# Keys and queries of an attention pair fetched and transposed earlier, and batch-end work moved by one slot

## Chip, cores and metric

One core of a Trainium2 chip runs the whole program. The metric is the device time of one execution, in microseconds (us); lower is better. The kernel before took 782.35 us (median of 3 runs, 782.05 to 782.71).

## What is computed

Three layers in a row, all in float32 at the interface. The change lies in the first; the batch ends belong to the second.

```python
# q, k, v: (4, 8, 1152, 64): 4 batches, 8 heads, 1152 positions, 64 channels
q_pool = q.reshape(B, H, S // 2, 2, D).mean(axis=3)          # 576 pooled queries a head
scores = (1 / sqrt(D)) * q_pool @ k.T
attn = softmax(scores, axis=-1)
x = (attn @ v)  -> (2304 tokens, 512)
logits = x @ phi                                             # soft mixture: 8 experts, 4 slots each
slot_in = softmax(logits, axis=0).T @ x
slot_out = relu(slot_in @ w1) @ w2                           # one w1, w2 per expert
y = softmax(logits, axis=1) @ slot_out
h = y @ w_in
out = where(h >= 1, h, where(h <= -1, 0, (h + 1)**2 / 4)) @ w_out
```

## The kernel before, in words

**Pairs, steps, slots.** The 32 heads are worked in 16 pairs (P = 0 to 15), two heads of one batch at a time. A pair has NK = 9 steps, one for each 128 keys, and each step has two slots (one per head, or per half). Global step g runs from -11 to 144; pair P's scores lie in steps 9P to 9P + 8. The main loop (L705 to L721) emits for each slot, in this order: one half block of maxima (`max_half`, L296), one block of transposed scores with its exponential (`st`, L361), the sums of exponentials where they are due (`es_sum`, L388, at steps 7 and 9 after the pair's start), one product with the values (`pv`, L397), and then whatever the plan has put into that slot (`slot`, L646). The order in which instructions are emitted is the order on each engine; the framework adds the waits, and a tile in a pool with one buffer is handed on when its last reader is done.

**Maxima run ahead.** The maxima of pair P are computed 11 steps (LEAD = NK + 2) before its scores, that is from step 9P - 11, slot 0, on. PE multiplies K1[P] with q1[P] (L305), VectorE (DVE) reduces (L317), and `max_fin` (L339) turns the maxima into the rows of q2[P], transposed by a DMA (L354). PE waits at the first L305 of a pair until K1[P] and q1[P], with its copy, are in place.

**The prologue of a pair** is what the change moves. For pair P, with b = 9P, `plan` (L584) puts:

- `load_k2` and `load_q` (L219, L231): two key loads (L229) and four query loads (L237 to L240), all issued by SP, into kf and qf;
- `prep_khi` (L249): ScalarE (ACT) makes the fp16 high part of the keys, one pass per head, in kn;
- `prep_klo` (L254): DVE makes the low part, the last reader of kf;
- `prep_qp`, `prep_qhi`, `prep_qlo` (L269, L275, L282): DVE adds the two neighbours of each pooled query, ACT makes the high part in qn1, DVE the low part; `prep_qlo` is the last reader of qf;
- `xpose_k` (L263): SP issues one DMA transpose per head, kn to K1 (L266);
- `xpose_q1` (L286): one DMA transpose, qn1 to q1 (L288);
- `dup_q1` (L290): a DMA copies the upper 64 rows of q1 to the lower 64 (L291), after the transpose has landed.

kf, qf, kn and qn1 have one buffer each (pool g0, `bufs=1`); K1 and q1 have three, by P % 3. The table PREP (L44) gives the steps for two plans: entries are load step, key high step, two key low half steps, pooled query half step, query high step, query low half step, all relative to b. The first plan serves pair 2, the second all later ones; pairs 0 and 1 are started by hand (L650 to L690).

```python
 44 PREP = (-20, -18, (-34, -33), -36, -16, -30), (-24, -22, (-41, -37), -41, -19, -37)
587     lk, hk, lok, aq, hq_, loq = PREP[P > 2]
```

A half step s means step s // 2, slot s % 2: -34 is (b - 17, 0), -30 is (b - 15, 0). Within a slot, pairs are planned in rising order.

**What shares the queues.** SP issues every DMA of this stage: also the value loads (L246, step b - 8, slot 1), the fill of S2 from K1 (L294, step b - 9, slot 1), the stores and loads of the weight conversion (L209, L212, L185), q2's transposes (L354), and, at the end of every ninth step from 30 on, a weight load of 1 MB (L133). SP works in order: what waits there holds all that is queued behind.

**Batch ends.** After every fourth pair the finished tokens give logits for the mixture: `lg_part`, `lg_sum`, `lg_max`, `lg_exp`, `lg_nat` (six small PE transposes and a DVE copy), `p_mm` (products with the tokens, PE) and `p_add` (DVE), at half steps LGT (L33) after b of the pair that ends the batch; for b = 63 half step 34 is (80, 0). The last batch has its own order and isn't touched. PE's results of scores, maxima and these share three PSUM tiles (pool sc, L73).

Of the kernel before, what the change touches and what calls it, by code (L numbers as in the profile page):

```python
# [29 lines left out]
P1G = -2, -1, 0, 1, 2, 3, 4, 5, 6  # L30
TMUL = (12, 0, 0, (0, 1)), (12, 1, 0, (2,)), (12, 1, 1, (0,)), (13, 0, 1, (1, 2))
TXN = 0, 1
LGT = 30, 31, 32, 33, 34, 36, 37  # L33
LPT = 6
WPH = 3
REA = 0
# [4 lines left out]
ADD = ((4, 1, 0, 0, 2), (5, 1, 1, 0, 1), (6, 1, 1, 1, 2), (6, 2, 0, 0, 2), (7, 2, 1, 0, 2), (8, 3, 0, 0, 1), (9, 3, 0, 1, 2),  # L41
       (10, 3, 1, 0, 2), (10, 4, 0, 0, 1), (11, 4, 0, 1, 2), (12, 4, 1, 0, 1), (13, 4, 1, 1, 2))

PREP = (-20, -18, (-34, -33), -36, -16, -30), (-24, -22, (-41, -37), -41, -19, -37)  # L44


@with_exitstack
def fused_kernel(ctx: ExitStack, tc: tile.TileContext, q, k, v, phi, w1, w2, w_in, w_out, out):
# [532 lines left out]
    def at(g, slot, f, *a):  # L581
        sched.setdefault((g, slot), []).append((f, a))

    def plan(P):  # L584
        b = NK * P
        if P > 1:
            lk, hk, lok, aq, hq_, loq = PREP[P > 2]
            for h in range(2):
                at(b + lk, 0, (load_k2, load_q)[h], P)
                at(b + hk, h, prep_khi, P, h)  # L590
                at(b + lok[h] // 2, lok[h] % 2, prep_klo, P, h)
                at(b - 17, h, xpose_k, P, h)
            at(b + aq // 2, aq % 2, prep_qp, P)
            at(b + hq_, 0, prep_qhi, P)
            at(b - 16, 0, xpose_q1, P)
            at(b + loq // 2, loq % 2, prep_qlo, P)
            at(b - 15, 1, dup_q1, P)
        if P > 0:
            at(b - 8, 1, load_v, P)
            at(b - 9 if P > 1 else 1, 1, s2_fill, P)  # L600
        for s, *a in ADD:
            at(b + s // 2, s % 2, es_add, P, *a)
        for h in range(2):
            at(b + 9, h, tail_raw, P, h)
            if h and P:
                at(b + 2, 0, tail_fin, P - 1)
            at(b + 9, h, tail_sum, P, h)
        for c, i, ns in TAT:
            pre[b + c, i] = P, ns
        last = P == NP - 1  # L610
        if not last:
            at(b + 11, REA, tail_rec, P)
        for i in range(2):
            at(b + (10 if last else 12), i if last else TXN[i], tail_xn, P, i)
            if last:
                at(b + 12, i, tail_mul, P, i)
        if not last:
            for c, sl, *a in TMUL:
                at(b + c, sl, tail_mul, P, *a)
        if last:  # L620
            at(b + 11, 0, tail_rec, P)
            at(b + 11, 0, tail_fin, P)
        at(b + 13 + (not last), last, tail_xt, P)
        if P % HPB == HPB - 1:
            q_ = P // HPB
            if last:
                at(b + LPT, 1, lg_part, q_)
                at(b + 11, 1, lg_half, q_)
                at(b + 14, 1, lg_sum, q_)
                at(b + 14, 1, warm, WARM[0])  # L630
                at(b + 14, 1, raw_mm, range(B - 1))
                at(b + 14, 1, warm, WARM[5])
                at(b + 15, 1, lg_max, q_)
                at(b + 15, 1, lg_exp, q_)
                at(b + 15, 1, lg_raw, q_)
                at(b + 16, 1, lg_nat, q_)
                at(b + 16, 1, warm, WARM[1])
                at(b + 18, 1, raw_mm, (B - 1,))
                at(b + 18, 1, warm, WARM[2])
                at(b + 17, 0, p_mm, q_)  # L640
                at(b + 17, 0, p_add, q_)
            else:
                for f, t in zip((lg_part, lg_sum, lg_max, lg_exp, lg_nat, p_mm, p_add), LGT):
                    at(b + t // 2, t % 2, f, q_)
# [9 lines left out]
    with tc.manual_schedule():  # L654
# [40 lines left out]
        for P in range(NP):  # L695
            plan(P)
# [8 lines left out]
        for g in range(-LEAD, nsteps + 1):  # L705
            mx = [divmod(g + LEAD, NK)] if not NK <= g + LEAD < 2 * NK else []
            mx += [(1, t) for t in range(NK) if P1G[t] == g]
            P, c = divmod(g, NK)
# [425 lines left out]
```

## Time and profile before

| | us |
|---|---|
| median of 3 runs | 782.35 (782.05 to 782.71) |
| profiled execution, whole | 787.7 |
| its span | 785.9 |
| PE busy in the span | 757.1 (96%) |
| DVE busy | 581.4 (74%) |
| ACT busy | 451.7 (57%) |
| share of the chain that ended last on PE | 60% |
| mean granted TensorE clock | 0.983 |

The profile is of one execution. Its times are microseconds from the start of the span; "L305" is line 305 of the kernel. A line of the trace gives start, duration, engine, line, operation, the tile written and the tile read, shapes and a count; in square brackets stands how long the engine had been idle before it and who released it. PE is the matmul engine, PEld its weight load, SPq the queue that SP issues DMAs from (its durations are issue times; the time from issue to landing is given per line). A granted clock of 1.00 is TensorE's 2.4 GHz, 0.50 its 1.2 GHz.

### The profile page before, as it was taken

Reading aid. Unit: us, or ns where it says so; the run is one execution under the profiler, and the core shown is the slowest. Engines: PE = TensorE matmul, PEld = TensorE weight load, DVE = VectorE, ACT = ScalarE, POOL = GpSimd, SP = SyncE. Lnnn points to the kernel's source line nnn. Section 1 sums busy time; section 2 is a strip of 40 time slices with the busy share of each in tenths; the row PEclk is TensorE's granted clock in tenths of the full one; section 3 lists DMA queues with packets and bytes.
Section 4 is the critical chain, followed back from the end, with each engine's and each line's share of the span. In section 5 each row is a group of like instructions: output and inputs, shape, how many; then the busy total and the mean of one; then the engine's idle time right before and its main releaser. Section 6 shows DMA issues by size and latency. Waiting matters only on the chain.

```text
span 785.9 us, 19049 instructions
## 1 busy us (share of the span) xinstructions
PE 757.1 (96%) x7896; PEld 556.6 (71%) x7896; DVE 581.4 (74%) x947; ACT 451.7 (57%) x855; POOL 125.9 (16%) x100
## 2 busy tenths in 40 slices
PE   7779999999999999999999999999789999999998
PEld 6557777766767766777766776633578888888887
DVE  6878999988989888999988793151697777666520
ACT  4246667676657565676675666401686777556620
POOL 7000000000000000000000000002574444443330
PEclk8889999999999999999999999999989999999999
DMA  8786788797788797799998836799600000000000
GB/s 215 201 174 137 182 193 205 206 248 200 186 233 203 183 260 164 188 263 180 212 263 134 222 96 237 269 333 395 241 0 28 28 28 20 7 28 28 27 28 28
DMA packets 138263, 127.11 MB, mean 162 GB/s; under 512 B 80576, under 2 KB 100288, under 8 KB 137408
## 3 DMA queue, kind: packets, MB, share of 16 engines
q1 hardware_dynamic: 138176, 125.89, 61.0%
q8 instruction: 62, 1.02, 0.6%
q14 instruction: 25, 0.20, 0.1%
HBM read 87.10 MB, written 13.11 MB: 128 GB/s over the span
## 4 chain that ended last, share of the span: by engine, by line
PE 60%; DMA 2%; DVE 2%; ACT 2%; issue 1%; SPq 0%; ACTq 0%; DVEq 0%
PE acc L401 9%; PE st L371 9%; PE po L1031 8%; PE po L1032 8%; PE po L1033 8%; PE mx L305 4%; PE acc L394 3%; DMA wi<-wi_dr 2%; PE h L968 2%; PE h L775 2%; PE tx L439 1%; PE tb L466 1%; DVE r L1021 1%; PE tr L428 1%; PE lp L482 0%
## 5 line engine op out<-in xcount | busy, mean ns | idle before, releaser
L376 ACT ACTIVATE e<-st 128x576 f32<-128x576 f32 x288 | 187.0, 651 | 139.0 <-PE st L371 125.6
L317 DVE TENSOR_REDUCE mp<-mx 128x1 f32<-128x576 f32 x282 | 212.1, 754 | 44.9 <-PE mx L305 38.0
L401 PE MATMUL acc<-e,vf 128*64 128x288 f32 x1152 | 195.1, 411 | 0.5 <-ACT e L376 0.5
L305 PE MATMUL mx<-K,q 128*64 128x288 f16 x1152 | 124.8, 298 | 9.6 <-DVE mp L317 3.4
L371 PE MATMUL st<-q,K 128*64 128x288 f16 x1152 | 122.0, 288 | 5.9 <-ACT e L376 4.7
L371 PE MATMUL st<-q,S 128*64 128x288 f16 x1152 | 122.0, 287 | 0.0
L305 PEld LDWEIGHTS <-q 128*64 128x64 f16 x1152 | 66.3, 112 | 70.2 <-issue 24.5
L1031 PE MATMUL po<-whi,ghi 128*128 128x512 f32 (+1 forms) x280 | 108.5, 388 | 0.0
L1032 PE MATMUL po<-wlo,ghi 128*128 128x512 f32 (+1 forms) x280 | 108.5, 388 | 0.0
L1033 PE MATMUL po<-whi,glo 128*128 128x512 f32 (+1 forms) x280 | 108.0, 386 | 0.0
L981 DVE TENSOR_TENSOR r<-cl,r 128x1024 f32<-128x1024 f32 x34 | 80.6, 2372 | 36.9 <-ACT cl L980 36.9
L987 POOL TENSOR_TENSOR glo<-r,ghi 128x1024 fp32r<-128x1024 f32 x34 | 82.2, 2417 | 95.3 <-ACT ghi L986 95.3
L401 PEld LDWEIGHTS acc<-e,vf 128*64 128x64 f32 x1152 | 77.4, 137 | 8.3 <-ACT e L376 2.0
L371 PEld LDWEIGHTS <-K 128*64 128x64 f16 x1152 | 68.3, 110 | 20.9 <-issue 12.7
L752 POOL MEMSET xfer<- 128x1024 f32 x1 | 1.0, 957 | 493.5 <-PE pb L562 493.5
L384 DVE TENSOR_TENSOR es<-es,e 128x288 f32<-128x288 f32 (+1 forms) x144 | 77.5, 550 | 2.2 <-ACT e L376 2.2
L371 PEld LDWEIGHTS <-S 128*64 128x64 f16 x1152 | 69.3, 110 | 3.4
L971 ACT ACTIVATE r<-h,cols 128x512 f32<-128x512 f32 x68 | 43.0, 685 | 31.4 <-PE h L968 31.4
L1033 PEld LDWEIGHTS po<-whi,glo 128*128 128x128 f32 x280 | 53.2, 190 | 10.8
L1031 PEld LDWEIGHTS po<-whi,ghi 128*128 128x128 f32 x280 | 53.4, 191 | 9.8
L1032 PEld LDWEIGHTS po<-wlo,ghi 128*128 128x128 f32 x280 | 53.3, 190 | 9.3
L972 DVE TENSOR_SCALAR cl<-h 128x512 f32<-128x512 f32 x68 | 43.8, 685 | 15.8 <-ACT r L971 13.9
(191 smaller groups left out, 854.1 us busy)
## 6 DMA issues: line engine op xcount, KB each, us to landing
w<-in_moe_w_dram SPq DMA_DIRECT2D x31, 1024.0 KB, 7.9
vf<-in_v_dram SPq DMA_DIRECT2D x16, 576.0 KB, 6.1
kf<-in_k_dram SPq DMA_DIRECT2D x30, 288.0 KB, 4.1
f<-in_moe_w_out_dram SPq DMA_DIRECT2D x16, 512.0 KB, 5.1
f<-in_moe_w_in_dram SPq DMA_DIRECT2D x16, 512.0 KB, 5.5
qf<-in_q_dram SPq DMA_DIRECT2D x30, 256.0 KB, 4.9
S<-K SPq DMA_DIRECT2D x16, 288.0 KB, 5.6
out_dram<-ob SPq DMA_DIRECT2D x17, 256.0 KB, 2.0
```

Source lines behind the costliest of these rows:

```text
L305: nc.tensor.matmul(ps[p0:p1, i, 0:HQ], lhsT=q1[P][:, t, p0:p1], rhs=kk[:, j * HQ:(j + 1) * HQ], start=True, stop=True)
L317: nc.vector.tensor_reduce(out=mp[P][:, t, a:a + 1], in_=ps[:, :, 0:HQ], op=ALU.max, axis=AX.XY)
L371: nc.tensor.matmul(ps[c0:c0 + 64, i, 0:HQ], lhsT=kk[:, ci, c0:c0 + 64], rhs=f[:, sl[i]], start=first, stop=not first)
L376: nc.scalar.activation(out=e, in_=ps[:, :, 0:HQ], func=AF.Exp, scale=ESC)
L384: nc.vector.tensor_tensor(out=Es[P, n, h][:, i0:i1], in0=a[:, i0:i1], in1=b[:, i0:i1], op=ALU.add)
L401: nc.tensor.matmul(acc[P, i][h * 64:(h + 1) * 64, 0:HQ], lhsT=vt[P][:, h, c, :], rhs=E[P, c, h][:, i, :], start=(c == 0), stop=(c == NK - ...
L972: nc.vector.tensor_scalar(out=cl[:, a:b], in0=src, scalar1=-1.0, scalar2=1.0, op0=ALU.max, op1=ALU.min)
L981: nc.vector.tensor_tensor(out=r[:, sl], in0=cl[:, sl], in1=r[:, sl], op=ALU.add)
L987: nc.gpsimd.tensor_tensor(out=glo[n, qd][:, sl], in0=r[:, sl], in1=ghi[n, qd][:, sl].bitcast(F32), op=ALU.subtract)
L1031: nc.tensor.matmul(po, lhsT=ghi[n, qd][:, j, sl], rhs=whi[:, f, cs], start=(f == 0), stop=False)
L1032: nc.tensor.matmul(po, lhsT=ghi[n, qd][:, j, sl], rhs=wlo[:, f, cs], start=False, stop=False)
L1033: nc.tensor.matmul(po, lhsT=glo[n, qd][:, j, sl], rhs=whi[:, f, cs], start=False, stop=(f == 15))
```

## The change

```diff
-LGT = 30, 31, 32, 33, 34, 36, 37
+LGT = 30, 31, 32, 33, 35, 37, 38
...
-PREP = (-20, -18, (-34, -33), -36, -16, -30), (-24, -22, (-41, -37), -41, -19, -37)
+PREP = (-20, -18, (-34, -33), -36, -16, -30), (-26, -22, (-41, -37), -41, -19, -37)
...
         if P > 1:
-            lk, hk, lok, aq, hq_, loq = PREP[P > 2]
+            lk, hk, lok, aq, hq_, loq = PREP[P > 3]
             for h in range(2):
                 at(b + lk, 0, (load_k2, load_q)[h], P)
                 at(b + hk, h, prep_khi, P, h)
                 at(b + lok[h] // 2, lok[h] % 2, prep_klo, P, h)
-                at(b - 17, h, xpose_k, P, h)
+                at(b - 17 - (P > 3), h, xpose_k, P, h)
             at(b + aq // 2, aq % 2, prep_qp, P)
             at(b + hq_, 0, prep_qhi, P)
-            at(b - 16, 0, xpose_q1, P)
+            at(b - 16 - (P > 3), 0, xpose_q1, P)
             at(b + loq // 2, loq % 2, prep_qlo, P)
-            at(b - 15, 1, dup_q1, P)
+            at(b - 15 - (P > 3), 1, dup_q1, P)
```

For pairs 4 to 15 the loads go from step b - 24 to b - 26, the key transposes from b - 17 to b - 18, the query transpose from b - 16 to b - 17 and the copy from b - 15 to b - 16; the passes on ACT and DVE between them stay. Pair 3 goes from the second plan to the first: its loads from b - 24 to b - 20, its passes two to four steps later, its transposes and copy where they were. At the ends of batches 0 to 2 the transposes (`lg_nat`), the products (`p_mm`) and the sum (`p_add`) go one slot later.

## Rows read from the trace of the kernel before

**Rows 1.** The page, part 1: busy time, share of the span, instructions
```profile
PE 757.1 (96%) x7896; PEld 556.6 (71%) x7896; DVE 581.4 (74%) x947; ACT 451.7 (57%) x855; POOL 125.9 (16%) x100
```

**Rows 2.** Timeline, DVE: closing maximum of pairs 6, 7, 8 (start, duration, line)
```profile
202.74 0.17 DVE L350 TENSOR_TENSOR mm<-mp 128x9 f32<-128x9 f32 x1
...
230.49 0.17 DVE L350 TENSOR_TENSOR mm<-mp 128x9 f32<-128x9 f32 x1
...
259.16 0.17 DVE L350 TENSOR_TENSOR mm<-mp 128x9 f32<-128x9 f32 x1
```

**Rows 3.** Timeline, PE and ACT: waits at pairs 8, 9 and 11
```profile
231.35 0.14 PEld L305 LDWEIGHTS <-q 128*64 128x64 f16 x4 [1.23 <-DMA q<-q]
...
261.06 0.44 PE L305 MATMUL mx<-K,q 128*64 128x288 f16 x4 [1.76 <-issue]
...
287.13 0.68 ACT L252 ACTIVATE kn<-kf 128x576 f16<-128x576 f32 x1 [1.12 <-DMA kf<-in_k_dram]
...
288.40 0.19 PEld L401 LDWEIGHTS acc<-e,vf 128*64 128x64 f32 x2 [1.03 <-ACT e L376]
```

**Rows 4.** Timeline, SP's queue: key loads of pair 10, copy of pair 9
```profile
251.74 1.05 SPq L229 DMA_DIRECT2D kf<-in_k_dram  x2
...
255.11 1.20 SPq L291 DMA_DIRECT2D q<-q  x1
```

**Rows 5.** Timeline, SP, ACT and PE at the prologue of pair 3
```profile
43.88 3.22 SPq L288 DMA_TRANSPOSE q<-qn  x1
...
51.04 0.68 ACT L252 ACTIVATE kn<-kf 128x576 f16<-128x576 f32 x1 [3.07 <-DMA kf<-in_k_dram]
...
52.31 0.44 PE L371 MATMUL st<-q,K 128*64 128x288 f16 x4 [2.88 <-ACT e L376]
```

**Rows 6.** Stretches: length, busy time of PE, PEld, DVE, ACT, POOL; clock, DMA, GB/s
```profile
53.60:56.00 2.40, 1.37 (x12) 0.91 (x10) 1.47 (x5) 1.22 (x2) 0.00 (x0) 0.50 0.12 30
56.00:58.50 2.50, 2.50 (x20) 1.98 (x18) 1.72 (x3) 1.20 (x2) 0.00 (x0) 0.50 0.62 118
58.50:61.40 2.90, 2.90 (x57) 1.73 (x55) 0.70 (x2) 0.65 (x1) 0.00 (x0) 0.79 0.00 0
```

**Rows 7.** Timeline, PE and DVE from pair 2's maxima to pair 3's
```profile
65.10 0.41 PE L305 MATMUL mx<-K,q 128*64 128x288 f16 x4
...
74.28 0.41 PE L305 MATMUL mx<-K,q 128*64 128x288 f16 x4
...
75.77 0.75 DVE L384 TENSOR_TENSOR es<-es,e 128x576 f32<-128x576 f32 x1
...
85.12 0.41 PE L305 MATMUL mx<-K,q 128*64 128x288 f16 x4
...
86.34 0.41 PE L305 MATMUL mx<-K,q 128*64 128x288 f16 x4
```

**Rows 8.** Lines 266, 288, 291: issue ns min/median/max, time to landing
```profile
L266 SPq DMA_TRANSPOSE K<-kn x32: 1251/2048/3087, 5.4 to 425.6; - x32
...
L288 SPq DMA_TRANSPOSE q<-qn x16: 1298/2912/4232, 9.6 to 429.4; - x16
...
DMA to landing us min/median/max: 3.2/5.5/7.5
...
L291 SPq DMA_DIRECT2D q<-q x14: 472/540/1197, 50.5 to 436.1; - x14
...
DMA to landing us min/median/max: 2.2/4.5/5.9
```

**Rows 9.** Timeline, PE at the end of batch 1: steps 80 and 81
```profile
296.79 0.41 PE L305 MATMUL mx<-K,q 128*64 128x288 f16 x4
...
298.68 0.44 PE L305 MATMUL mx<-K,q 128*64 128x288 f16 x4
...
299.39 0.44 PE L371 MATMUL st<-q,K 128*64 128x288 f16 x4 [0.28 <-DVE mp L317]
...
300.36 0.44 PE L305 MATMUL mx<-K,q 128*64 128x288 f16 x4
```

## The prediction

> **What bounds the kernel now.** I read the page's busy times first. TensorE (PE) is busy for 96% of the span [rows 1], so a change off PE pays only where PE stands still or runs at its lower clock. The next view is the start of the small maximum that closes each pair's maxima: pair 7 takes 27.75 us from pair 6 (230.49 - 202.74), pair 8 takes 28.67 [rows 2]. 27.75 is the undisturbed pair; what lies above it in a pair without a batch end is waiting. Third, the idle times in front of single instructions. PE starts the maxima of pair 8 after a weight-load idle of 1.23 on the q copy, and those of pair 9 after 1.76 without work. The key pass of pair 11 on ScalarE (ACT) waits 1.12 for its load, and PE then 1.03 for the exponentials behind it [rows 3]. Fourth, the SyncE queue (SP) in that stretch: six loads of pair 10 are issued from 251.74, and the copy for pair 9, which PE waits for until 261.06, goes out only behind them, at 255.11 [rows 4]. Last, the start: the key passes of pair 3 hold ACT for 3.07, PE is idle 2.88 [rows 5], and the granted clock falls to 0.50, the 1.2 GHz level, until about 59 [rows 6].
>
> Rows are of the profiled execution, 787.7 us (span 785.9 and 1.8 around it); the median of the runs shown is 782.35, 5.35 less. I sum against 787.7 and carry the difference to the median. A measurement of this kernel can tell about 0.2% (1.6 us) from no change.
>
> **Part 1, pairs 4 to 15: loads two steps, transposes and copy one step earlier.** No instruction is added; for each pair SP issues the same six loads, three transposes and one copy. Their order among themselves barely changes: the copy of pair P still stands behind the six loads of pair P + 1, and now behind one value load more, but the whole chain begins a step earlier, two plain slots of 1.22 (86.34 - 85.12 [rows 7]), so 2.4, less 0.5 for that load's issue [rows 4]. The copy of pair 9 has to come 1.76 earlier, that of pair 8 at most 1.23: both are covered, by little, if the landings stay as they are. The weight loads of 1 MB at the end of every ninth step, which went out right behind the copy, now stand a step behind it. The key load for pair 11 is two steps earlier; it was 1.12 late. Removed: 0.92 for pair 8 (28.67 - 27.75), 1.76 + 1.03 for pair 9 and the load of pair 11; together 3.7. Nothing else is late in these pairs: the undisturbed 27.75 is PE's own work. The bound is 0 if the executions that are timed don't have these waits (they are 5.35 shorter), 3.7 if they do. The earlier K transposes wait for the last scores of pair P-3 one slot before, so that costs nothing.
>
> **Part 2, pair 3: its prologue now runs by the first plan, four steps later.** It follows from the index P > 3, which leaves P = 3 to the plan that pair 2 had. Removed is the stall at 49 to 61: 2.88 of idle [rows 5], 1.03 more idle (2.40 - 1.37), and the half clock, 1.37/2 + 2.50/2 + 2.90 x 0.21 = 2.5 [rows 6]. Sum 6.4. Next late there could be the copy of pair 2: its transposes are issued at 43.88 and SP is free at 47.10 [rows 5]; they land 5.5 after issue, at 49.4, and the copy 2.2 to 4.5 later [rows 8], 51.7 to 54.0. The maxima of pair 2 would start at 52.2 (86.34 - 6.4 - 27.75). I take 2.2, the row with nothing queued behind, so 0; the other end is +1.8. So without a new wait pair 3's maxima, which started at 86.34 [rows 7], would start at 79.9.
>
> **Part 3, the new wait.** kf and qf have one buffer. The loads of pair 4 stand at step 36 - 26 = 10, slot 0. By the first plan the last reader of pair 3's keys is the low split at (10,1), and of its queries the low split at (12,0). So the query load of pair 4 holds SP until VectorE (DVE) has done (12,0). Queued behind it on SP: the value load of pair 2, the second K transpose of pair 3, a store and a load of converted weights, the q transpose of pair 3 and its copy, which PE needs at (16,0). Worked out: (9,0) stood at 65.10 and (12,0) at 74.28 [rows 7], now 58.7 and 67.9. In (12,0) DVE is through its sums 2.24 after the start (75.77 + 0.75 - 74.28), and the split takes another such 0.75 pass: 70.9. Four such passes are new on DVE between (9,0) and (12,0), and the first may wait for its query load; I add 1.0 (bounds 0 and 3.0, all four uncovered): 71.9. SP then issues seven plain DMAs at 0.53 (half of the 1.05 for two) [rows 4], 3.7, and one K transpose, 2.05 (1.25 to 3.09) [rows 8]: the q transpose goes out at 77.7. It lands 5.5 later (3.2 to 7.5), 83.2; the copy follows at once and lands 2.2 to 5.9 later, median 4.5 [rows 8]. Nothing is issued behind it meanwhile, so I take 3.0, near the low row: **86.3**. That is where it started before (86.34): the whole 6.4 of part 2 is given back. Low end: 1.0, 0.8, 2.3 and 0.8 less, about 81.4; high end 2.0, 1.0, 2.0 and 2.9 more, 94.2. On the way ACT waits too: the key pass of pair 4 writes the one kn buffer that the delayed K transpose reads. That wait ends before the copy lands, so it isn't added.
>
> The Trainium skill says (DMA: Bandwidth & Descriptors, Queues, rings and completion order) that each DMA engine takes descriptors in ring order. This speaks against the change: loads hurried ahead in SP's order would also stand ahead of the late transposes in the rings, not on SP alone. No row of the kernel before shows that order by itself; by it the landing would lie toward 7.5, which the rival below prices.
>
> **The clock.** Idle of 2.88 was followed by 0.50 [rows 5, 6]; after idle of 1.76 four matmuls took 0.44 against a plain 0.41 [rows 3, 7], no fall. PE loses about 6 here in two pieces, so it probably falls again: between 0 and the 2.5 of rows 6. Half is spent while PE would wait anyway; I take 1.3. The Trainium skill has the same two levels (TensorE: Matmul & The Clock Gate, What's actually happening), the lower one as the default that activity lifts; the trace agrees, with 0.50 after the wait and 0.79 on the way back. By it the fall would be certain and the sum 1.2 worse.
>
> **Part 4, batch ends (three).** Transposes, products and the sum go one slot later; same instructions on PE, DVE and ACT, no DMA. In batch 1 the two slots from 296.79 take 1.89 and 1.68 against the plain 1.22, and the scores wait 0.28 for DVE's maximum [rows 9]. That wait comes from DVE standing behind the exponential, which is not moved; so at most 0.28 in each of two batches is gained, -0.6. Against it, the copy out of the transposes now comes just before two split passes of 0.75 on DVE; if PE waits for one, 0.75 per batch, 2.2 in all. I take +0.4, near no change, since the work is the same.
>
> **Sum:** -3.7 (part 1), -6.4 + 6.4 (parts 2 and 3), +1.3, +0.4 = -2.0. 785.7 against 787.7, and 780.3 on the median.
>
> **Rivals.** (a) Forecast, 0.42: slightly faster, 780.3.
> (b) Slower, 0.29: the held query load decides. Place: the first maxima matmul of pair 3, at (16,0). With landings 7.5 and 5.9, 77.7 + 7.5 + 0.1 + 5.9 = 91.2, 4.9 later than before, and the whole clock fall 2.5: 4.9 + 2.5 - 3.7 + 0.4 = +4.1, 786.4. It decides from a start of pair 3 at 88.3 on, 2.0 late. For it: such landings occur [rows 8], and the seven plain DMAs of the burst are still under way then. Against: SP issues nothing more while it waits for the transpose, so the copy finds little in front of it.
> (c) No change, 0.25: the waits of pairs 8, 9 and 11 are half there in the shorter executions that are timed: -2.0 + 1.85 = -0.2, 782.2. For it: they depend on landings late by 1 to 2, and the timed runs are 5.35 shorter. Against: the SP order that makes them is fixed.
> (d) The new wait doesn't exist, 0.04 (were the early load given another buffer): pair 3 starts at 79.9, -6.4 - 3.7 + 0.4 = -9.7, 772.6. One buffer per tag excludes it nearly.
>
> **Numbers.** Faster 0.42 + 0.04 less a little of (a) that stays within 0.2%: 0.44. Within: 0.27. Slower: 0.29. The range goes from 776.2 (the forecast less half of part 3's low end, 2.5, the clock's 1.3 and half of part 4's gain, 0.3) to 786.4 (rival b); (d) and the ends of (b) are the 2 in 10 left out. Cases of both signs hold most of the chance; (a)'s own range is 778 to 782.
>
> **What would show it.** Right: no ACT wait for kf near 50 and clock 1.00 there; a long SP wait in front of pair 4's query loads that ends with DVE's split, pair 3's copy issued after 80, a PE idle of several us in front of pair 3's first maxima; pairs 8 and 9 at 27.75 and near 29; batch ends as before within 0.7. Wrong: pair 3 starting near 80 (then far faster), or near 91 with half clock (slower), or waits on the q copy left in later pairs.

## The result, and the profile after

The changed kernel takes 789.38 us (median of 4, 788.1 to 791.42), the kernel before beside it 782.2 (median of 4, 781.37 to 782.71): ratio 1.009, interval 1.007 to 1.0111. It is slower by 7.2 us, where 2 us faster was forecast; the time lies above the range, and it goes the way of rival (b).

The profiled execution took 791.42 us, the longest of the four, its span 789.6, at a mean granted clock of 0.985. The page of the changed kernel, part 1:

```profile
PE 758.5 (96%) x7896; PEld 556.1 (70%) x7896; DVE 580.4 (74%) x947; ACT 450.9 (57%) x855; POOL 125.7 (16%) x100
```

Shares (within one per cent) and counts are as in [rows 1]: what is lost lies in a few waits, so the reading goes on by pairs. The timeline of the changed kernel, DVE: closing maximum of pairs 1, 2 and 3 (the rows that answer to [rows 2]):

```profile
51.86 0.17 DVE L350 TENSOR_TENSOR mm<-mp 128x9 f32<-128x9 f32 x1
...
84.08 0.17 DVE L350 TENSOR_TENSOR mm<-mp 128x9 f32<-128x9 f32 x1
...
116.90 0.17 DVE L350 TENSOR_TENSOR mm<-mp 128x9 f32<-128x9 f32 x1
```

Pair 2 takes 32.22, pair 3 takes 32.82, against 27.75 undisturbed. What makes them long is read from SP's queue in that stretch (start, issue time, line, operation):

```profile
66.48 0.80 SPq L229 DMA_DIRECT2D kf<-in_k_dram  x2
72.09 0.38 SPq L237 DMA_DIRECT2D qf<-in_q_dram  x1
...
74.89 1.31 SPq L266 DMA_TRANSPOSE K<-kn  x1
...
77.87 2.29 SPq L288 DMA_TRANSPOSE q<-qn  x1
85.13 0.50 SPq L291 DMA_DIRECT2D q<-q  x1
```

The waits of that queue from 62 to 90 (waiting line, releaser: us in total, times, longest), and in the timeline of PE and ACT the idle times behind them:

```profile
SPq L291 <- DMA q<-qn: 4.9, 1, 4.9
...
SPq L237 <- DVE qn L283: 4.7, 1, 4.7
```
```profile
81.03 0.68 ACT L252 ACTIVATE kn<-kf 128x576 f16<-128x576 f32 x1 [2.36 <-DMA K<-kn]
82.30 0.13 PEld L401 LDWEIGHTS acc<-e,vf 128*64 128x64 f32 x1 [2.27 <-ACT e L376]
82.30 0.46 PE L401 MATMUL acc<-e,vf 128*64 128x288 f32 x1 [1.76 <-ACT e L376]
...
87.60 0.69 PE L305 MATMUL mx<-K,q 128*64 128x288 f16 x4 [3.38 <-issue]
```

Pair 4's query load (L237) stands 4.7 at the head of SP's queue until DVE has split pair 3's queries (L283). Pair 3's second key transpose and its query transpose go out behind it, at 74.89 and 77.87, the copy at 85.13; it lands 2.4 later, and PE starts pair 3's maxima at 87.60. The key transpose also keeps the kn buffer from ACT, whose exponentials then keep PE waiting: its weight loads for 2.27, its matmuls for 1.76. The windows show the start without its stall and the clock after the new one (length, busy time of the engines, granted clock, DMA share, GB/s):

```profile
47.50:53.60 6.10, 6.02 (x80) 4.26 (x80) 6.03 (x13) 3.50 (x6) 0.00 (x0) 1.00 0.24 49
53.60:61.40 7.80, 7.80 (x144) 5.81 (x135) 4.72 (x9) 3.50 (x6) 0.00 (x0) 1.00 0.90 230
84.00:87.60 3.60, 0.22 (x1) 0.03 (x1) 2.08 (x6) 0.43 (x1) 0.00 (x0) 0.97 0.53 114
87.60:90.00 2.40, 2.40 (x27) 1.60 (x31) 1.09 (x2) 0.65 (x1) 0.00 (x0) 0.50 0.41 79
90.00:93.00 3.00, 3.00 (x62) 2.24 (x56) 0.45 (x1) 0.00 (x0) 0.00 (x0) 0.87 0.00 0
```

The half clock of [rows 6] has moved from 54 to 87.6: 2.40/2 + 3.00 x 0.13 = 1.6 us are lost to it there.

### The profile page after: what moved, and what is told of

Read it like the earlier page. It is cut to its first block, busy times and chain, and to the rows that moved or that the text cites. A ratio compares the mean times of both kernels' runs of the same rounds, so it can differ in the third digit from the quotient of the medians.

```text
span 789.6 us, 19077 instructions
## 1 busy us (share of the span) xinstructions
PE 758.5 (96%) x7896; PEld 556.1 (70%) x7896; DVE 580.4 (74%) x947; ACT 450.9 (57%) x855; POOL 125.7 (16%) x100
## 4 chain that ended last, share of the span: by engine, by line
PE 82%; DVE 7%; DMA 5%; ACT 2%; issue 2%; SPq 2%; ACTq 0%; DVEq 0%
PE st L371 16%; PE acc L401 16%; PE mx L305 8%; PE po L1031 8%; PE po L1032 8%; PE po L1033 8%; PE acc L394 5%; DVE mp L317 3%; DMA wi<-wi_dr 2%; PE h L968 2%; PE h L775 2%; PE tx L439 2%; DMA q<-qn 1%; PE tb L466 1%; DMA qf<-in_q_dram 1%
```

## The experiments

Each kernel was timed beside the kernel before on the same chip. The table gives the median, the ratio to the kernel before with its 95% interval, and from each profiled execution the lengths of some pairs (differences of the starts of L350; 6 and 14 hold a batch end). Runs without an interval were executed once.

| run | us | ratio | 2 | 3 | 6 | 8 | 9 | 12 | 14 |
|---|---|---|---|---|---|---|---|---|---|
| before, profiled execution | 787.7 | | 31.11 | 27.75 | 31.61 | 28.67 | 32.25 | 27.76 | 32.96 |
| after | 789.38 | 1.009 [1.007, 1.0111] | 32.22 | 32.82 | 31.94 | 27.76 | 29.07 | 29.53 | 33.28 |
| e0 before again | 783.62 | 1.0013 [0.9998, 1.0029] | 29.37 | 27.76 | 31.60 | 28.76 | 29.83 | 28.23 | 32.96 |
| e1 pair 3 old | 785.06 | 1.0037 [1.002, 1.0053] | 28.43 | 29.01 | 31.94 | 27.75 | 29.08 | 29.41 | 33.29 |
| e2 no hold | 781.54 | 0.9988 [0.997, 1.0005] | 29.95 | 27.76 | 31.93 | 27.75 | 29.09 | 28.77 | 33.28 |
| e3 new list only | 784.9 | 1.0029 [1.0015, 1.0044] | 30.28 | 27.76 | 31.95 | 28.31 | 31.67 | 27.75 | 33.28 |
| e4 pair 3 only | 780.5 | 0.9975 [0.9959, 0.999] | 29.89 | 27.75 | 31.60 | 28.15 | 29.07 | 27.76 | 32.95 |
| e5 no hold, old list | 781.85 | 0.9986 [0.9972, 1.0] | 29.86 | 27.76 | 31.61 | 27.75 | 29.09 | 29.76 | 32.96 |
| e6 hold only | 788.48 | 1.0075 [1.0054, 1.0097] | 32.17 | 34.76 | 31.61 | 28.98 | 29.48 | 27.90 | 32.96 |
| e7 later pairs only | 784.15 | 1.0019 [1.0004, 1.0034] | 28.95 | 29.09 | 31.60 | 27.76 | 29.09 | 28.64 | 32.95 |
| e8 own buffer | 783.65 | 1.0019 [1.0004, 1.0033] | 30.24 | 28.34 | 31.94 | 27.75 | 29.08 | 27.76 | 33.30 |
| e9 loads only | 785.69 | | 29.08 | 28.75 | 31.61 | 29.36 | 29.77 | 27.90 | 32.96 |
| e10 transposes only | 782.65 | | 28.85 | 27.76 | 31.41 | 28.70 | 30.14 | 27.76 | 32.81 |
| e11 products only | 783.01 | | 29.13 | 27.76 | 32.14 | 28.92 | 29.10 | 27.76 | 33.44 |
| e12 pair 3, transposes | 780.66 | 0.9964 [0.9947, 0.9981] | 29.78 | 27.75 | 31.39 | 29.13 | 29.70 | 29.17 | 32.80 |
| e13 values after copy | 780.26 | 0.9954 [0.9938, 0.9971] | 29.81 | 27.75 | 31.95 | 27.75 | 29.08 | 27.75 | 33.29 |
| e14 mended | 777.84 | 0.9935 [0.9914, 0.9955] | 29.82 | 27.76 | 31.40 | 27.76 | 29.08 | 27.75 | 32.82 |

The theory H is that the held query load is the loss. Its rivals stand in the expectations.

**e0, the kernel before again.** No edit. 

> The kernel before, unchanged. It took 787.7 us when profiled and 782.2 when timed. Theory A (the waits of pairs 3, 8, 9 and 11 in that one profile are not in a usual execution): ratio 1.000, and a profile of a usual execution of about 782 shows pair 9 within 1 us of pair 5 (29.1) and pair 3's stall near 50 shorter than 6.4. Theory B (they are always there): the profile shows pair 8 at 28.7 and pair 9 at 32 again, and the 5.4 us lie elsewhere.

The 35 executions of before that were timed with e0 to e3 lie between 780.17 and 786.68; the profiled one that the prediction was worked from, 787.7, lies above all of them. The profile of e0 shows the same stall at the start, but a smaller one (timeline of ACT and PE, then the windows that answer to [rows 6]):

```profile
50.06 0.68 ACT L252 ACTIVATE kn<-kf 128x576 f16<-128x576 f32 x1 [1.67 <-DMA kf<-in_k_dram]
51.33 0.44 PE L371 MATMUL st<-q,K 128*64 128x288 f16 x4 [1.48 <-ACT e L376]
```
```profile
47.50:53.60 6.10, 4.55 (x56) 3.26 (x52) 4.30 (x9) 3.17 (x6) 0.00 (x0) 1.00 0.97 250
53.60:61.40 7.80, 6.75 (x114) 4.96 (x112) 5.82 (x12) 3.59 (x6) 0.00 (x0) 1.00 0.22 43
```

PE idles 1.48 where [rows 5] have 2.88, and the clock stays at 1.00 where [rows 6] have 0.50: the stall that the change takes away was large in that one execution. PE then starts pair 3's maxima 3.4 earlier than in [rows 7] (timeline of PE):

```profile
82.92 0.41 PE L305 MATMUL mx<-K,q 128*64 128x288 f16 x4
```

So theory A holds for pair 3's stall and for pair 9, which is within 1 us of pair 5 (29.83 and 29.63); pair 8 is late as before (28.76), as theory B has it. Since e0 has no edit, its 1.0013 also says how little a ratio that near to 1 means.

**e1, the change with pair 3 on its old plan.**

```diff
-PREP = (...), (-26, -22, (-41, -37), -41, -19, -37)
+PREP = (...), (-24, -22, (-41, -37), -41, -19, -37), (-26, -22, (-41, -37), -41, -19, -37)
-            lk, hk, lok, aq, hq_, loq = PREP[P > 3]
+            lk, hk, lok, aq, hq_, loq = PREP[(P > 2) + (P > 3)]
```

> The change with pair 3 left on its old plan (loads at b - 24, transposes and copy unmoved either way); pairs 4 to 15 and the batch ends as changed. The query load of pair 4 then comes after pair 3's last reader. Theory H (the held query load makes the loss): the new wait in front of pair 3's maxima is gone, about 782 to 783, ratio 0.998 to 1.002 against the kernel before. Theory L (the batch ends and the later pairs make it): still 787 or more, ratio over 1.006.

1.0037: most of the loss is gone, but not all; the ratio lies between the two theories' ranges. Without pair 3's move there is no hold (L237 waits 0.3 on SP instead of 4.7). But pair 3 lasts 29.01: pair 4's loads still stand in SP's queue ahead of pair 3's second key transpose and its query transpose (see e7).

**e2, the change without the hold.**

```diff
             lk, hk, lok, aq, hq_, loq = PREP[P > 3]
+            if P == 4:
+                lk = -24
```

> The change with one number altered: pair 4's loads at b - 24 (step 12, slot 0, right behind pair 3's last query reader) instead of b - 26; pair 3 on the first plan as changed. Theory H: SP is not held, pair 3's copy goes out about 6 us earlier and its maxima start near 80 to 81 instead of 87.6, no half clock behind: 9 us less than the change in a profile, and 780 or less in time, ratio under 0.998. Theory L: pair 3's start moves, but the time stays over 785.

0.9988: with one pair's loads back, 1% returns, a little less than theory H asked for (under 0.998). Pair 3 lasts 27.76. SP's queue in e2, and the start of pair 3's maxima on PE:

```profile
69.88 1.91 SPq L288 DMA_TRANSPOSE q<-qn  x1
71.85 1.06 SPq L229 DMA_DIRECT2D kf<-in_k_dram  x2
...
75.57 0.51 SPq L291 DMA_DIRECT2D q<-q  x1
```
```profile
81.96 0.41 PE L305 MATMUL mx<-K,q 128*64 128x288 f16 x4
```

The query transpose now goes out ahead of pair 4's loads, 8.0 earlier than in the change (77.87 - 69.88), and the copy 9.6 earlier.

**e3, the new list of batch-end slots alone**, in the kernel before.

```diff
-LGT = 30, 31, 32, 33, 34, 36, 37
+LGT = 30, 31, 32, 33, 35, 37, 38
```

> The kernel before with the batch-end list alone changed. The two profiles differ there by 0.33 us in each of three batches. Theory H: +1.0, ratio 1.000 to 1.002. Theory L: at least half of the 7 us, ratio over 1.004.

1.0029, slower, between the two theories' ranges. In the trace pairs 6 and 14 (and 10 alike) are longer by 0.32 to 0.35, about 1.0 in all, that is 0.13%; the rest of the ratio isn't explained.

**e4, pair 3's move alone**, in the kernel before.

```diff
-            lk, hk, lok, aq, hq_, loq = PREP[P > 2]
+            lk, hk, lok, aq, hq_, loq = PREP[P > 3]
```

> The kernel before, with pair 3's steps put on the first plan that pairs 0 to 2 have (its loads and transposes leave the start of the pipeline and fall into pair 2); all other pairs and the list of transposes as before. Theory H (the change's loss is pair 4's query load holding SP's queue until pair 3's queries are transposed, and that hold is absent here because pair 4 still loads late): the start gets shorter and nothing is late, 778 to 781 us, ratio 0.994 to 0.999; pair 3 lasts 27.8 us. Rival M (moving pair 3's steps is itself what makes pair 3 late, hold or no hold): pair 3 lasts 31 us or more, 784 to 788 us, ratio above 1.002.

0.9975, 780.5. Pair 3 lasts 27.75, so the move itself makes nothing late; rival M falls.

**e5, the change without the hold and with the old list.** The two lines of e2, and LGT as before. 

> The change with two things taken back: pair 4's loads go out two steps later than the change puts them (after pair 3's query transposes, so that nothing holds SP), and the list of batch-end transposes and token products is the old one. If the hold and the list are the whole loss and add up: the run without the hold (ratio 0.9988) less the 0.0029 of the list alone gives 0.996, about 779 us. If the later pairs' earlier steps cost something of their own in this arrangement (the wait in pair 12 seen in the other runs with the first half of the change): 781 to 783 us, ratio 0.998 to 1.001.

0.9986, the second case: pairs 7 and 12 last 28.88 and 29.76. So the earlier steps of the later pairs cost something of their own. Both pairs wait for their query copy: it takes 8.6 and 8.1 to land, 1.0 and 1.9 after the closing maximum of the pair before.

**e6, the hold alone:** e4, with pair 4's loads two steps earlier.

```diff
             lk, hk, lok, aq, hq_, loq = PREP[P > 3]
+            if P == 4:
+                lk = -26
```

> The run that moves only pair 3's steps, and in it pair 4's loads two steps earlier, so that its query load stands in SP's queue ahead of pair 3's second set of transposes; nothing else differs. Theory H: the hold alone costs what it costs in the change, 7 to 9 us over the run that moves only pair 3's steps, 786 to 789 us, ratio 1.004 to 1.009; pair 3 lasts 32 us or more and its first maxima start near 87 us. Rival M, or a loss that lies with the later pairs: no more than 1 us between these two runs.

788.48 against 780.5 for e4 on the same chip: 8.0 us for moving six loads of one pair by two steps. SP's queue in e6, and the closing maxima of pairs 2 and 3:

```profile
66.81 0.81 SPq L229 DMA_DIRECT2D kf<-in_k_dram  x2
72.42 0.38 SPq L237 DMA_DIRECT2D qf<-in_q_dram  x1
...
78.75 1.59 SPq L288 DMA_TRANSPOSE q<-qn  x1
86.17 0.50 SPq L291 DMA_DIRECT2D q<-q  x1
```
```profile
84.17 0.17 DVE L350 TENSOR_TENSOR mm<-mp 128x9 f32<-128x9 f32 x1
...
118.93 0.17 DVE L350 TENSOR_TENSOR mm<-mp 128x9 f32<-128x9 f32 x1
```

The same chain as in the change to about 1 us, with none of its other parts: L237 waits 4.7 here too. Pairs 2 and 3 are 2.3 and 7.0 longer than in e4; in the change they are 2.3 and 5.1 longer than in e2. Of the 1.9 between 7.0 and 5.1, 1.1 is clock: the lower level lasts longer here and costs 5.36/2 = 2.7, against 1.6 in the change (window, with the granted clock behind the counts):

```profile
88.64:94.00 5.36, 5.36 (x64) 3.54 (x66) 1.09 (x2) 0.65 (x1) 0.00 (x0) 0.50 0.18 36
```

**e7, the later pairs alone:** e1 with the old list. 

> The kernel before with only pairs 4 to 15 loaded two steps and transposed one step earlier; pair 3 and the list of transposes as before. From the two runs on record (the change with pair 3 on its old plan, 1.0037, less the list alone, 1.0029): ratio 1.000 to 1.002, about 783 us, that is, nothing gained where the forecast had 3.7 us from the waits of pairs 8, 9 and 11. If those waits do cost what the profile of before showed: ratio 0.995 to 0.997, 778.5 to 780 us.

1.0019: nothing gained; a loss isn't clear, with e0 at 1.0013. Against e0's trace, gains of 2.7 in pairs 5, 8, 9 and 13 stand against 1.3 in pair 3, 1.2 in pair 7 and 0.4 in pair 12. Pairs 7 and 12 wait for copies that take 8.6 and 7.1 to land. Pair 3, whose own steps are as before, is held back by pair 4's six loads, which now go out ahead of its second key transpose and its query transpose: its copy goes out at 81.61, in e0 at 78.34. SP's queue and PE at pair 3, then PE at pair 7, in e7:

```profile
81.61 0.51 SPq L291 DMA_DIRECT2D q<-q  x1
84.02 0.44 PE L305 MATMUL mx<-K,q 128*64 128x288 f16 x4 [1.14 <-ACT e L376]
...
201.57 0.44 PE L305 MATMUL mx<-K,q 128*64 128x288 f16 x4 [1.07 <-ACT e L376]
```

**e8, the whole change, with a buffer of its own for pair 4's queries.**

```diff
-        qf = g0.tile([128, NK, 2, D], F32, tag="qf", name=f"qf{P}") ...
+        qf = g0.tile([128, NK, 2, D], F32, tag="qf" if P != 4 else "qf4", name=f"qf{P}") ...
```

> The whole change, but pair 4's queries are loaded into a buffer of their own, so that the load need not wait until pair 3's queries have been read; the order of everything on every engine and queue is that of the change. Theory H (the wait for the buffer, standing at the head of SP's queue, is the loss): the loss of the hold goes away though the load stands exactly where the change puts it; pair 3 lasts 27.8 us, about 781.5 us, ratio 0.997 to 1.0005, as in the run that moves the load back. Rival T (what delays pair 3's transposes is the earlier load itself: five more issues ahead of them on SP and its packets beside theirs): most of the loss stays, 786 to 790 us, ratio 1.005 or more, pair 3 at 31 us or more.

783.65, 1.0019, between the two theories' ranges. The load stands where the change has it, but needn't wait:

```profile
67.00 0.83 SPq L229 DMA_DIRECT2D kf<-in_k_dram  x2
67.88 1.49 SPq L237 DMA_DIRECT2D qf<-in_q_dram  x1
...
75.33 1.84 SPq L288 DMA_TRANSPOSE q<-qn  x1
80.26 0.50 SPq L291 DMA_DIRECT2D q<-q  x1
```

The copy goes out 4.9 earlier than in the change (85.13 - 80.26), pair 3 lasts 28.34 instead of 32.82, and by the ratios 5.6 us return (1.009 - 1.0019 = 0.0071). So the wait is most of the loss, and not the load's own issue and packets. A rest does go rival T's way: the load's issues stand ahead of pair 3's transposes, the query transpose goes out 5.4 later than in e2 (75.33 - 69.88), and pair 3 is 0.6 longer. The ratio lies 0.003 above e2's, on another chip; in the two profiled executions pair 15 closes within 0.3 of the same time (462.75 and 463.05), so the traces don't tell where the rest of that is.

**e9, the later pairs' loads alone**, without their transposes and copies. The PREP lines of e1 in the kernel before; the lines with b - 17, b - 16 and b - 15 stay. 

> The kernel before with pairs 4 to 15 only loaded two steps earlier; their transposes and copies stay where they were. One look, for the lengths of pairs in the trace. If the wait of about 1.3 us that pair 12 shows in every run with the later pairs moved (28.6 to 29.8 us against 27.8 to 28.2 without) comes from the earlier transposes and copy meeting other transfers, it is absent here and pair 12 lasts 27.8 to 28.2 us; if from the earlier loads, it is here too. The 0.8 us that pair 8 gains (27.8 against 28.2 to 28.9) should stay if the load was what was late there, and go if the copy was. Time 781 to 784 us.

Pair 12 is 27.90 and pair 8 is 29.36: the loss of pair 12 and the gain of pair 8 both come with the earlier transposes and copies, as far as one execution tells, and not with the loads. The time, 785.69, is above the 781 to 784 expected: pairs 3, 10 and 13 last 28.75, 34.02 and 30.82, each 1.0 to 1.3 more than in e0, pair 3 as in e7. The copies themselves land fast here, where the six loads and the value load have gone out two steps ahead of them (time to landing over all 14, min/median/max):

```profile
DMA to landing us min/median/max: 2.3/2.4/4.6
```

What happens at pair 12 is seen in the change (SP's queue, the closing maximum of pair 11, PE's next maxima; then the time to landing of that copy, min/median/max of one):

```profile
344.41 0.38 SPq L246 DMA_DIRECT2D vf<-in_v_dram  x1
345.13 0.51 SPq L291 DMA_DIRECT2D q<-q  x1
...
351.45 0.17 DVE L350 TENSOR_TENSOR mm<-mp 128x9 f32<-128x9 f32 x1
...
353.17 0.44 PE L305 MATMUL mx<-K,q 128*64 128x288 f16 x4 [1.58 <-issue]
```
```profile
DMA to landing us min/median/max: 8.0/8.0/8.0
```

and for e4, with the old steps:

```profile
339.86 0.54 SPq L291 DMA_DIRECT2D q<-q  x1
```
```profile
DMA to landing us min/median/max: 3.6/3.6/3.6
```

In e4 the copy goes out 3.9 before the closing maximum of pair 11 (at 343.72) and lands 0.3 before it. In the change it goes out 6.3 before, 2.5 earlier, but right behind a value load of 576 KB (and a weight load of 512 KB ahead of that), takes 8.0, and lands 1.7 after: PE waits 1.58. Over all 14 copies the median landing is 7.0 in the change and 4.9 in e4.

**e10 and e11, the two halves of the list**, in the kernel before.

```diff
+LGT = 30, 31, 32, 33, 35, 36, 37      (e10: transposes)
+LGT = 30, 31, 32, 33, 34, 37, 38      (e11: products and their sum)
```

> The kernel before with only the batch-end transposes one slot on (34 to 35); the token products and their addition stay. One look, for the lengths of pairs 6, 10 and 14. If the transposes make the 0.33 us that each of these pairs gains with the whole new list, they last 31.9, 33.3 and 33.3 us; if the products do, 31.6, 32.95 and 32.95 us as before. Time 781 to 785 us.

> The kernel before with only the token products and their addition one slot on (36, 37 to 37, 38); the batch-end transposes stay. One look, the other half of the list: pairs 6, 10 and 14 at 31.6, 32.95 and 32.95 us if the transposes make the 0.33 us, at 31.9, 33.3 and 33.3 us if the products do. Time 781 to 785 us.

Closing maxima of pairs 5 and 6 in e10, then in e11:

```profile
168.59 0.17 DVE L350 TENSOR_TENSOR mm<-mp 128x9 f32<-128x9 f32 x1
...
200.00 0.17 DVE L350 TENSOR_TENSOR mm<-mp 128x9 f32<-128x9 f32 x1
```
```profile
167.40 0.17 DVE L350 TENSOR_TENSOR mm<-mp 128x9 f32<-128x9 f32 x1
...
199.54 0.17 DVE L350 TENSOR_TENSOR mm<-mp 128x9 f32<-128x9 f32 x1
```

31.41 and 32.14 against 31.60: neither of the two cases expected. In pair 6 the transposes gain 0.19 and the products lose 0.54, and the list's 0.33 is their sum.

**e12, e4 with the transposes of e10.** 

> The kernel before with pair 3's steps on the first plan and only the batch-end transposes one slot on (34 to 35): the two parts that gained in the runs so far. If both hold and add up: pair 3 at 27.8 us, pairs 6, 10 and 14 at 31.4, 32.8 and 32.8 us (0.15 to 0.2 us each under before), 780 us, ratio 0.996 to 0.998. If the transposes' gain was chance: the three pairs at 31.6, 32.95 and 32.95 us, ratio as with pair 3 alone, 0.9975.

0.9964; pairs 6 and 14 are 31.39 and 32.80, as expected. Pairs 8, 9 and 12 are late again in its profile (29.13, 29.70, 29.17), with the waits of the old steps: in pair 12 a key pass on ACT waits 1.32 for its load, as the one in [rows 3] does.

**e13, e2 with the value load behind the copy.**

```diff
-            at(b - 8, 1, load_v, P)
+            at(b - (6 if P > 2 else 8), P < 3, load_v, P)
```

> The change without the hold (pair 4's loads two steps later), and from pair 3 on the value load two steps later, so that it stands behind the copy of the next pair's queries in SP's queue instead of ahead of it; nothing else differs. If the copy's 7 to 8 us came from the value load ahead of it: the copies land in about 3.6 us, pair 12 lasts 27.8 us, and the time is about 1 us under that of the run without the hold, 780 to 781.5 us, ratio 0.997 to 0.999. If the copy is slow for other traffic: it takes 6 us or more, pair 12 stays at 28.6 us or more, ratio 0.9985 to 1.0005.

0.9954, better than expected. The copy at pair 12 lands in 6.0, not in the 3.6 expected (a weight load of 512 KB still goes out 0.4 ahead of it), but that is less than the 8.4 of e2, the median of all copies falls to 4.8 (6.5 in e2), and no pair waits for one: pair 12 lasts 27.75, and pairs 3, 7, 8, 11 and 15 are at 27.75 or 27.76 too.

**e14, e13 with only the transposes of the list moved** (35, 36, 37). 

> The run with the value load behind the copy, and of the batch-end list only the transposes moved (35, 36, 37): the change with its three losses taken out, the earlier steps of all pairs from 3 on kept. If the losses are those three and no others: pairs 6, 10 and 14 at 31.4, 32.8 and 32.8 us, pairs 3, 7, 8 and 12 at 27.8 us, 778.5 to 780 us, ratio 0.995 to 0.9975, at or below the run that moves only pair 3's steps. If the later pairs' earlier steps still cost or give nothing: the same as the run with only pair 3's steps and the transposes moved, within 0.001, or above it.

777.84, 0.9935 [0.9914, 0.9955]: 5.6 us under the kernel before beside it (783.45), the fastest of all and better than expected. The ratio is 0.003 under that of e12, which leaves the later pairs' steps as before (the intervals overlap a little), so the change's idea seems to hold once its three losses are out. One rival is not tested: the later value load alone, with the old steps, may make part of that gain.

## Why the prediction was wrong, point by point

**Part 3, the new wait: right.** Forecast was SP held until 71.9, the query transpose at 77.7, PE's start at 86.3; the trace has 72.09, 77.87 and 87.60. The 1.3 too little comes from the query transpose: the copy could follow only at 85.13, 7.3 after it, where 5.5 was taken; rival (b) had 7.5. The copy then took 2.4, where 3.0 was taken, but not for the reason given. The prediction tied short landings to nothing being queued behind; the copy of 2.2 in [rows 8], the last one of before, has weight loads of 1 MB right behind it (SP's queue in before):

```profile
436.07 0.47 SPq L291 DMA_DIRECT2D q<-q  x1
436.65 1.13 SPq L133 DMA_DIRECT2D w<-in_moe_w_dram  x2
```

What it lacks is loads right ahead, as in e9. The wait of ACT for kn, seen but not added, lengthened pair 2 by 2.27 (32.22, in e2 29.95). Against e2, where pair 3's maxima start at 81.96, the start is 5.6 late; with the 1.6 of clock that is 7.2, and e6 less e4 measures 8.0. Rival (b) was right that the held load decides, but its condition, a start from 88.3 on, was not met: 87.60 was enough, since the gains set against it were smaller.

**Part 2, the step that failed first.** The text said of the forecast start, "That is where it started before (86.34): the whole 6.4 of part 2 is given back". That can hold at most for one execution, 787.7, the longest of before that was seen. In e0 pair 3's maxima start at 82.92, not at 86.34 [rows 7]. Without the hold they start at 81.96 (e2), not at the 79.9 forecast: pair 2 was taken at 27.75 and lasts 29.95 there. So against e0 the start comes 1.0 earlier, and pair 3's move alone is worth 782.7 - 780.5 = 2.2 us (e4), not 6.4. The stall ahead depends on when a key load lands and shrank to 1.48 of idle at full clock (e0); the hold behind it comes from the order of SP's queue and is 4.7 in both traces that have it (the change, e6). Set against each other, the two come near cancelling only in the longest execution. The 5.35 between that execution and the median were named at the start of the prediction, but carried over as a constant; most of them lay in the very stalls that were counted as gains: against e0's trace, pair 15 of the longest execution closes 4.5 later (469.67 - 465.22), with 3.4 lost in pairs 0 to 2 and 2.4 in pair 9, and the others 1.4 shorter. Rival (c) had this for part 1, not for part 2.

**Part 1: mechanism right, a term missing.** Pairs 8 and 9 do lose their waits (27.76 and 29.07 in the change). By e0 these were 1.0 and 0.8, not the 0.92 and 2.79 of the sum. What was missed stands in the words "and now behind one value load more", priced at its issue, 0.5. Its packets cost more: the copy behind it took 8.0 instead of 3.6, and pair 12 waits. Alone the part measures 1.0019 (e7), 1.5 us slower by the medians where a gain of 3.7 was forecast: what pairs 5, 8, 9 and 13 gain, pairs 3, 7 and 12 lose. For pairs 7 and 12 it is the copy's place behind the value load: e13 moves only that load, and no copy is waited for. Pair 3's 1.3 is rival T's effect, and in the change it is part of the hold. The Trainium skill (DMA: Bandwidth & Descriptors, Queues, rings and completion order) says that each DMA engine takes descriptors in ring order; the prediction weighed that against part 3 and not here. The landings agree with it: medians of 2.4 with nothing right ahead (e9), 4.5 behind the six loads (before, [rows 8]) and 7.0 with the value load right ahead too (the change). That the order within a queue is the reason no row shows.

**The clock: right.** 1.6 against 1.3, inside the bounds of 0 and 2.5; in e6 it is 2.7, just above them.

**Part 4: sign right, size short.** +1.0 in the traces (0.33 in each of three batches) against +0.4, inside the bounds given. The products make it, 0.5 a batch, and not the copy out of the transposes, as was argued: the transposes alone gain (e10, e11).

**The sum.** Forecast and measured, in us: part 1 -3.7 and +1.5 (e7), part 2 -6.4 and -2.2 (e4), part 3 with the clock +7.7 and +8.0 (e6 less e4), part 4 +0.4 and +1.0 (traces). So it is the gains of parts 1 and 2 that failed, not the loss. The measured terms add to 8.3; e7's 1.3 in pair 3 is in the hold's 8.0 already, and without it they give 7.0, measured 7.2. By the ratios of these runs: 0.9975 (e4), 1.0100 for the hold (1.0075 / 0.9975), 1.0029 (e3), 1.0019 (e7): together 1.0123, without pair 3's 1.3 (0.0017) 1.0106, measured 1.009 with an interval to 1.0111. The list is the other term that sticks out, by ratio more than by the traces: in three other pairs of runs, e2 and e5, e1 and e7, e13 and e14, it weighs 0.0002, 0.0018 and (products only) 0.0019. By the traces, after against e0, the closing of pair 15 is 5.9 later (471.10 - 465.22): pairs 0 and 1 -1.7, pair 2 +2.9, pair 3 +5.1, pairs 4 to 15 -0.3. In that last figure gains of 2.8 in pairs 5, 8, 9 and 13 stand against 1.3 in pair 12, 1.0 at the batch ends and 0.1 in pair 7. Another 1.0 of the two spans (789.6 and 782.7) lies behind pair 15, where nothing was changed.

## What to carry to other kernels

Before a load is moved ahead in an in-order queue, find the last reader of the buffer that it fills: if that reader is later than the load's new place, the wait stands at the head of the queue and delays everything behind it, here for 8 us; another buffer, or two steps less, takes it away. A gain that comes from a wait on a transfer is to be sized over several executions, since it varied here from 1.48 to 2.88 of idle, while the hold, which comes from an order, was 4.7 both times; and a small transfer sent earlier can land later when the new place is right behind a large one.

## What was not expected of the hardware

A copy between two halves of one tile, issued 2.5 us earlier, landed 1.9 us later in the schedule, because it took 8.0 instead of 3.6 behind a load of 576 KB. With no load right ahead such copies took 2.4 (e9), though loads of 1 MB went out right behind them. And a PE idle of 1.48 left the granted clock at 1.00 (e0), while an idle of 1.76 and then one of 3.38 were followed by 0.50 (the change), as the one of 2.88 in [rows 5] was.
